# A written order of smaller steps, SyncE's transfers included, for stages 2 and 3 of a two-layer attention and expert kernel

## Chip, cores and metric

One core of one Trainium2 chip. The metric is device microseconds of one launch. Three runs of the kernel before took 717.27 to 718.21 us, median 718.05.

## What is computed

Two rounds over x of 2048 rows and 576 columns, each a linear attention block and then a block of 64 experts, both behind a layernorm and added to x. The reference, cut:

```python
    def _A_ref(x, wqkv, wo):                      # H = 32 heads of 18
        q, k, v = ...(x @ wqkv)
        phi = lambda t: jnp.where(t > 0, t + 1, jnp.exp(t)) + 1e-6
        pq, pk = phi(q), phi(k)
        kv = jnp.einsum("bhsd,bhse->bhde", pk, v)
        z = jnp.einsum("bhsd->bhd", pk)
        o = einsum(pq, kv) / (einsum(pq, z) + 1e-6)
        return o.reshape(B, S, D) @ wo
    def _B_ref(x, w_q, k1, k2, u, v):             # H = 32, E = 8, 64 experts
        s1, s2 = (q1 @ k1.T), (q2 @ k2.T)         # q = x @ w_q, two halves of 128
        top_e = argmax(s1) * E + argmax(s2)       # per row and head
        act = gelu(einsum("nd,nhkd->nhk", x, u[top_e]))
        return einsum("nhk,nhkd->nd", act, v[top_e])
    x = x + _A_ref(_layernorm(x), A_wqkv, A_wo)
    x = x + _B_ref(_layernorm(x), ...)
    (both once more)
```

## The kernel before

The rows are 16 tiles of 128. Every matmul's operands are split into a rounded part `hi` and a remainder `lo` (`split`, L117: ScalarE rounds at L119, VectorE subtracts at L120), so that a product of 576 columns is 28 matmuls.

The work of one tile in one round, by the names that the order uses: `ln` or the end of `po` makes the normalised row; `fT` turns and splits it; `k`, `v`, `q` are products (`product`, L260) with their activations (`phi`, L276; in the second round `phi_scalar`, L283); `st` adds the tile to the state `kva` (L362). When all 16 tiles are in, `wl` loads wo, `mk`, `zs` and `M` mask the state, sum it into `zb` and fold it into wo (L381 to L437). Then per tile: `ld` loads x and phi(q) (L438, L443; parts `ldx`, `ldq`), `num` scales phi(q) (L455 to L465), `oT` turns and splits it, `O` is the output product (L485) with residual (L475) and layernorm (L189 to L207), `bT` turns and splits that, `S` are the expert scores (L527), `gel` and `sel` the gelu and the choice of experts (L541 to L590), `cT` turns the weights, and `po` is the expert output (L609) with residual and, in round one, the next layernorm; it stores x (L617) or the result (L623). In round two `bc` joins `bT` of one tile with `cT` of another. `keep` stores a turned tile to DRAM (L335, L336) and `rl` loads it again (L342, L343) for `lq`, the late q.

Turning goes in one of two ways. `transposed` (L209) uses TensorE (L217) and PSUM. `squares`, for the tiles listed in `SQUARES` (23 of `fT`, 10 of `oT`, 9 of `bT`), turns 32 by 32 squares on VectorE (`moved`, L231), writes them to DRAM (L233), reads them back in four transfers (L239) and splits what arrives.

There are three stages. Stage 1, an ordinary loop, does tiles 0 to 9 of the first `fT` to `st` and folds the expert keys. Stages 2 and 3 are written out by hand. A step of a piece of work is the code between two `yield`s of its generator; `play` reads a text such as `oT0.7x2` (two steps of `oT`, round 0, tile 7) and calls the steps in that order, and `in_order` (L159) then ties every instruction of TensorE, ScalarE, VectorE and GpSimd to the one before it on its engine. SyncE, which issues all DMAs, is not tied: the Tile scheduler chooses its order. The middle of stage 2 is a loop of one text over tiles in pairs (s = 5, 7, 9, 11). Buffers are taken when a step asks for them: four PSUM tiles (one of them the state), four pairs `hi`/`lo`, six `x1`, three `x`, three `y`, four `e` (phi of k and q).

Of the kernel before, what the change touches and what calls it, by code (L numbers as in the profile page):

```python
# [64 lines left out]
def network(ctx, tc, x_in, wqkv, wo, wq_t, k_t, u_t, v2, c_mask, c_mask4, c_ident, c_code, c_code1, c_scale, c_shift, out):  # L65
# [120 lines left out]
    def spread(xt, total, n):  # L186

        m = wk.tile([P, 2], F32, tag="mv", name=f"m{n}")
        nc.gpsimd.tensor_scalar(m[:, 0:1], total, -1.0 / D, 1.0, op0=ALU.mult, op1=ALU.mult)  # L189
        nc.scalar.activation(junk, xt, AF.Square, bias=m[:, 0:1], accum_out=m[:, 1:2])  # L190
        return m

    def layernorm_sum(xt, m, n):
        rs = wk.tile([P, 2], F32, tag="rs", name=f"rs{n}")
        nc.gpsimd.tensor_scalar(rs[:, 0:1], m[:, 1:2], 1.0 / D, EPS_LN, op0=ALU.mult, op1=ALU.add)
        nc.gpsimd.tensor_tensor(rs[:, 0:1], rs[:, 0:1], mhalf, op=ALU.pow)
        nc.gpsimd.tensor_tensor(rs[:, 1:2], m[:, 0:1], rs[:, 0:1], op=ALU.mult)  # L197
        return normalized(xt, rs, n)
# [11 lines left out]
    def transposed(y, n, more=None, tag="t", step=P):  # L210
# [16 lines left out]
    def moved(y, n, step=P):  # L227
# [3 lines left out]
        nc.vector.transpose(r.rearrange("p (j b c) -> p b j c", j=4, b=NB), at)  # L231
        d = dr.tile([P, NB * P], F32, name=f"y_d{n}")
# [9 lines left out]
    def squares(y, n, step=P):  # L242
        g = yield from moved(y, n, step)
        hi, lo = (wk.tile([P, NB, P], F32R, tag="t" + w, name=f"t{w}{n}", bufs=4) for w in ("hi", "lo"))
        yield
        split(g.rearrange("p q (b c) -> p b q c", b=NB), *(x.rearrange("p b (q c) -> p b q c", q=4) for x in (hi, lo)))
        return hi, lo
# [28 lines left out]
    def phi(p, n):  # L276
        e = wk.tile([P, D], F32, tag="e", name=f"e{n}", bufs=4)
        nc.scalar.activation(e, row(p), AF.Exp)  # L278
        nc.vector.tensor_scalar(e, e, 1.0, EPS, op0=ALU.min, op1=ALU.add)  # L279
        nc.vector.scalar_tensor_tensor(e, row(p), 0.0, e, op0=ALU.max, op1=ALU.add)  # L280
        return e

    def phi_scalar(p, n):  # L283
# [4 lines left out]
        nc.scalar.activation(e, e, AF.Exp, scale=-1.0)  # L288
        nc.vector.scalar_tensor_tensor(e, e, EPS, row(p), op0=ALU.add, op1=ALU.add)  # L289
# [13 lines left out]
    def front_k(l, t):  # L303
# [4 lines left out]
        tt["fk", l, t] = (phi_scalar if l else phi)(k, f"k{l}_{t}")  # L308
# [15 lines left out]
    def front_q(l, t):  # L324
# [4 lines left out]
        fq = phi(q, f"q{l}_{t}")  # L329
        nc.sync.dma_start(pq_d[l][t], fq)  # L330

    def front_keep(l, t):

        hi, lo = tt["f", l, t]
        nc.sync.dma_start(hl_d[t][:, 0], hi.bitcast(F32))  # L335
        nc.sync.dma_start(hl_d[t][:, 1], lo.bitcast(F32))  # L336

    def late_load(l, t):
# [3 lines left out]
        nc.sync.dma_start(hi.bitcast(F32), hl_d[t][:, 0])  # L342
        nc.sync.dma_start(lo.bitcast(F32), hl_d[t][:, 1])  # L343
        tt["f", l, t] = hi, lo

    def late_q(l, t):
        q = product(tt["f", l, t], whi, wlo, 0, f"q{l}_{t}")
        yield
        tt["pq", l, t] = phi_scalar(q, f"q{l}_{t}")
# [16 lines left out]
    def wo_load(l, t):  # L366
# [7 lines left out]
        yield  # L374
# [4 lines left out]
    def state_mask(l, t):  # L379
        a = kva.pop(l)  # L380
        nc.scalar.activation(zc, a[:, :4 * 72 + 36], AF.Copy)  # L381
        for h in range(2):
# [63 lines left out]
    def back_load(l, t):  # L446
        back_x(l, t)
        back_pq(l, t)

    def back_scale(l, t):  # L450
# [7 lines left out]
        nc.vector.tensor_reduce(den, o[:, :D].rearrange("p (h e) -> p h e", h=H), axis=AX.X, op=ALU.add)  # L458
        nc.gpsimd.tensor_scalar(den, den, EPS, 1.0, op0=ALU.add, op1=ALU.mult)
# [4 lines left out]
                                r.unsqueeze(2).to_broadcast([P, H, DH]), op=ALU.mult)  # L464
        nc.gpsimd.tensor_copy(o[:, D:D + 56], o[:, D - 56:D])  # L465
        tt["o", l, t] = o

    def back_oT(l, t):
        hi, lo = tt["oT", l, t] = yield from turned("o", l, t, tt.pop(("o", l, t)), HC)
        nc.gpsimd.tensor_copy(lo[96:112, 4], hi[:16, 4].bitcast(F32))  # L470
# [7 lines left out]
    def back_out(l, t):  # L478
# [11 lines left out]
        m = spread(x1, total, "b" + n)  # L490
        yield
        ys["b", l, t] = layernorm_sum(x1, m, "b" + n)
# [18 lines left out]
    def exp_c(l, t):  # L511
# [5 lines left out]
        split(pt[:, :P], hi, lo)  # L517
        tt["c", l, t] = hi, lo

    def exp_scores(l, t):  # L520
# [8 lines left out]
        s = wk.tile([P, D], F32, tag="s", name="s" + n)  # L529
        nc.gpsimd.memset(s[:, :NE], 0.0)  # L530
# [4 lines left out]
    def exp_gelu(l, t):  # L535
# [5 lines left out]
        nc.scalar.activation(g[:, 0], xu, AF.Square, scale=float(np.sqrt(0.044715)))  # L541
        nc.gpsimd.tensor_scalar(g[:, 0], g[:, 0], 1.0, 1.0, op0=ALU.add, op1=ALU.mult)
        nc.gpsimd.tensor_tensor(g[:, 1], g[:, 0], xu, op=ALU.mult)
        yield
        nc.scalar.activation(g[:, 1], g[:, 1], AF.Tanh, scale=GELU_C)
        nc.gpsimd.tensor_scalar(g[:, 1], g[:, 1], 1.0, 0.5, op0=ALU.add, op1=ALU.mult)
# [53 lines left out]
    def exp_out(l, t):  # L600
# [13 lines left out]
        else:  # L614
            x2, total = residual(p, xs.pop(("b", l, t)), n, "x2")
        if l == 0:
            nc.sync.dma_start(x_d[t], x2)  # L617
# [62 lines left out]
    def first_ln(l, t):  # L680
        xt = xs.pop(("f", t))
        *_, rs = statistics(xt, f"f0_{t}")
# [22 lines left out]
    def load_vu(l, t):  # L705
        sv = stage("vst")
        nc.sync.dma_start(sv[:64], v2)
        nc.sync.dma_start(sv[64:], v2)
        su = stage("ust")[:, :NB * NE].rearrange("p (b e) -> p b e", b=NB)
# [76 lines left out]
    with in_order(*ALL):  # L786
# [46 lines left out]
        for t in range(2, FIRST):  # L833
# [3 lines left out]
            if t == 2:  # L837
                first_load(0, 4)
                first_ln(0, 3)
# [13 lines left out]
            first_ln(0, t + 2)  # L853
# [5 lines left out]
    with in_order(*ALL):  # L859

        play("""
            fT0.11 v0.10 k0.10 fl0.13 v0.10 q0.10 ln0.13 v0.10 ln0.12 fT0.11x2 fT0.12 fl0.15 k0.10 fo0.3x2 lv0.0 q0.10
            v0.11 fT0.13 fT0.12 k0.11 v0.11x2 wl0.0 q0.11 ln0.15 k0.11 st0.11 fl0.14 fT0.13 st0.10 fT0.12 q0.11 ld0.1
            ln0.14 k0.12x2 v0.12x2 ld0.0 v0.12 fT0.13 q0.12 q0.13 fT0.14 q0.12 k0.13 fT0.14 v0.13 fT0.15 fT0.14 fT0.15
            k0.14 q0.13 k0.13 v0.13 fT0.15 k0.14 v0.13 st0.12 v0.14 k0.15 v0.15 st0.13 ld0.2 v0.14x2 st0.14 k0.15
            sv0.0 v0.15x2 st0.15 ld0.3 mk0.0 zs0.0x2 num0.0 M0.2x2 num0.1 M0.3x2 q0.14 num0.0 num0.1 M0.1 num0.0 oT0.0
            num0.1 M0.0 M0.4 oT0.1 M0.1 oT0.0 M0.0 M0.4 O0.0 num0.2x2 oT0.1 O0.0x3 ld0.4 num0.2 O0.1x2 oT0.2 ld0.5
            num0.3 bT0.0 num0.4 oT0.2 O0.2 ld0.6 num0.3 bT0.0 O0.1 S0.0 num0.3 num0.4 q0.14 O0.1 oT0.3 O0.2 S0.0 bT0.1
            O0.2 q0.15 gel0.0 num0.4 sel0.0 oT0.3 bT0.1 ld0.7 sel0.0x2 O0.2 S0.1 gel0.0 q0.15 num0.5 sel0.0 S0.1
            sel0.1 gel0.1 O0.3 gel0.1 sel0.1 cT0.0 bT0.2 cT0.0 O0.3 oT0.4 po0.0x2 bT0.2 sel0.1 S0.2 po0.0 oT0.4 O0.4  # L870
            sel0.1 S0.2 cT0.1 sel0.2 po0.0 sel0.2 fT1.0 gel0.2 cT0.1 fT1.0 O0.3 po0.1 gel0.2 sel0.2 po0.1 O0.3 v1.0
            sel0.2 cT0.2 po0.1 bT0.3 O0.4x2 cT0.2 k1.0 v1.0 po0.1 v1.0 fT1.1 num0.5 num0.6 bT0.3 k1.0 S0.3 po0.2 fT1.1
            po0.2 S0.3 sel0.3 keep1.0 sel0.3 k1.1 gel0.3 sel0.3 gel0.3 po0.2 k1.1 v1.1 O0.4 bT0.4 sel0.3 cT0.3 po0.2
            v1.1x2 fT1.2 num0.5 cT0.3 bT0.4 oT0.5 fT1.2 num0.6 oT0.5 S0.4x2 keep1.1 num0.6 oT0.6x2 O0.5 keep1.2 po0.3
            O0.5x3 st1.0 st1.1
        """)
    with in_order(*ALL):
# [8 lines left out]
    with in_order(*ALL):  # L886

        play("""
            bT0.13 gel0.12 po0.11 sel0.12 v1.10 po0.11x2 gel0.12 num0.15 sel0.12 k1.10 bT0.13 v1.10 sel0.12 fT1.11
            sel0.12 oT0.14 v1.10 fT1.11 O0.14 num0.15 cT0.12 num0.15 k1.10 cT0.12 O0.14 oT0.15 bT0.13 po0.12 S0.13  # L890
            O0.14 fT1.11 S0.13 oT0.15 po0.12x3 sel0.13x2 v1.11 gel0.13 fT1.12 gel0.13 oT0.15 O0.14 sel0.13x2 k1.11
            v1.11 O0.15 fT1.12 O0.15 bT0.14 st1.10 cT0.13 v1.11 bT0.14 S0.14 cT0.13 O0.15 fT1.12 keep1.12 po0.13 k1.11
            S0.14 gel0.14 sel0.14 po0.13 gel0.14 st1.11 po0.13 k1.12 sel0.14x2 po0.13 fT1.13 k1.12 O0.15 v1.12x2
# [74 lines left out]
```

## Time and profile before

| | |
|---|---|
| median of three runs | 718.05 us |
| the profiled execution | 716.96 us |
| its span | 715.1 us |
| busy: TensorE, VectorE, ScalarE, GpSimd | 698.0, 467.9, 321.7, 202.4 us |
| mean granted TensorE clock | 0.997 |
| moved by DMA | 107.17 MB, 150 GB/s mean |

In the profile PE is TensorE, PEld its weight loads, DVE VectorE, ACT ScalarE, POOL GpSimd and SPq SyncE's queue. An operand's name loses its buffer number: `thio` is a `hi` tile of `oT`, `go` the squares read back for it, `y_do` their copy in DRAM, `ppo` the PSUM of O. "Idle before" is the time in which an engine did nothing ahead of an instruction, with what ended it. A row of the waits gives total, number of times and longest in us. A row of the chain of waits or of the timeline gives start, duration and what ran.

### The profile page before, as it was taken

The numbers are of one execution on the slowest core, as the hardware profiler recorded it, in microseconds if no ns is written. First come the engines' busy times: TensorE is split into PE (matmuls) and PEld (weight loads), VectorE is DVE, ScalarE is ACT, GpSimd is POOL, SyncE is SP. The second block draws the span as 40 slices with busy tenths as digits, with TensorE's granted clock in tenths as the row PEclk, the third lists the DMA queues.
The fourth block names the chain that finished last, engine by engine and source line by source line (L and its number), as shares of the span: only waits on it lengthen the run. The fifth ranks groups of instructions, "written<-read, shape, count | busy, mean of one in ns | idle before, by whom it ended". The sixth has DMA issues, their size and how long they took to land.

```text
span 715.1 us, 14670 instructions
## 1 busy us (share of the span) xinstructions
PE 698.0 (98%) x5464; PEld 650.7 (91%) x5464; DVE 467.9 (65%) x1005; ACT 321.7 (45%) x658; POOL 202.4 (28%) x544
## 2 busy tenths in 40 slices
PE   9999999999999999999999999999999999999995
PEld 6999989999998899889998999999899999999984
DVE  5533342435436876688877888552647788987986
ACT  5422432343224547455555555544543544444443
POOL 2211000111004533333443433210224244433441
PEclk9999999999999999999999999999999999999998
DMA  9848878775302322566767675513632324121101
GB/s 269 293 153 255 267 229 264 247 196 176 108 1 53 114 91 93 166 209 210 233 207 241 216 220 175 165 53 100 176 98 82 123 71 137 45 73 34 67 17 66
DMA packets 82711, 107.17 MB, mean 150 GB/s; under 512 B 8976, under 2 KB 47376, under 8 KB 82640
## 3 DMA queue, kind: packets, MB, share of 16 engines
q1 hardware_dynamic: 82640, 106.24, 47.5%
q8 instruction: 43, 0.70, 0.4%
q14 instruction: 28, 0.23, 0.1%
HBM read 68.88 MB, written 37.32 MB: 149 GB/s over the span
## 4 chain that ended last, share of the span: by engine, by line
PE 79%; DVE 8%; ACT 4%; DMA 3%; issue 3%; POOL 1%; SPq 1%; DVEq 0%; ACTq 0%; POOLq 0%
PE ppq L260 15%; PE ppk L260 13%; PE ppo L485 13%; PE ppv L260 12%; PE pps L527 8%; PE kva L527 4%; PE kva L362 2%; PE fold_ps L641 2%; PE ptb L217 2%; PE po L609 2%; DMA go<-y_do 1%; PE m L416 1%; PE pto L217 1%; DVE x L475 1%; PE ppq L272 1%
## 5 line engine op out<-in xcount | busy, mean ns | idle before, releaser
L485 PE MATMUL ppo<-ohi,thio 126*128 126x252 f32 (+1 forms) x320 | 50.7, 301 | 4.5 <-ACT thio L119 4.4
L485 PEld LDWEIGHTS ppo<-ohi,thio 126*128 126x128 f32 (+1 forms) x320 | 44.9, 189 | 6.2 <-ACT thio L119 5.1
L260 PE MATMUL ppk<-whi,thif 128*128 128x252 f32 (+1 forms) x300 | 45.3, 298 | 0.8 <-ACT thif L119 0.8
L455 POOL TENSOR_TENSOR o<-pq,zb 128x576 f32<-128x576 f32 x19 | 27.4, 1443 | 62.5 <-ACT zb L401 58.7
L190 ACT ACTIVATE junk<-x,mb 128x576 bf16<-128x576 f32 x32 | 24.8, 775 | 45.0 <-POOL mb L189 44.9
L260 PE MATMUL ppv<-whi,thif 128*128 128x252 f32 (+1 forms) x300 | 44.7, 296 | 0.2 <-ACT thif L119 0.2
L260 PEld LDWEIGHTS ppk<-whi,thif 128*128 128x128 f32 x300 | 40.9, 188 | 4.0 <-issue 2.9
L181 POOL TENSOR_SCALAR rsf<-mvf 128x1 f32<-128x1 f32 x16 | 3.4, 212 | 145.3 <-DVE mvf L178 145.2
L207 ACT ACTIVATE yb<-x,rsb 128x640 f32<-128x640 f32 x32 | 29.5, 922 | 33.2 <-POOL rsb L197 33.2
L260 PE MATMUL ppv<-whi,tlof 128*128 128x252 f32 (+1 forms) x300 | 43.9, 293 | 0.0
L260 PE MATMUL ppk<-whi,tlof 128*128 128x252 f32 (+1 forms) x300 | 43.9, 293 | 0.0
L260 PEld LDWEIGHTS ppv<-whi,thif 128*128 128x128 f32 x300 | 41.4, 188 | 1.1 <-issue 0.4
L260 PEld LDWEIGHTS ppk<-whi,tlof 128*128 128x128 f32 x300 | 41.2, 188 | 0.0
L260 PEld LDWEIGHTS ppv<-whi,tlof 128*128 128x128 f32 x300 | 41.2, 188 | 0.0
L485 PE MATMUL ppo<-olo,thio 126*128 126x252 f32 (+1 forms) x256 | 39.6, 293 | 0.0
L260 PE MATMUL ppq<-whi 128*128 128x252 f32 (+1 forms) x260 | 39.5, 298 | 0.0
L485 PE MATMUL ppo<-ohi,tloo 126*128 126x252 f32 (+1 forms) x256 | 39.5, 293 | 0.0
L279 DVE TENSOR_SCALAR ek<-ek 128x576 f32<-128x576 f32 x16 | 7.3, 457 | 45.8 <-ACT ek L278 45.6
L260 PEld LDWEIGHTS ppq<-whi 128*128 128x128 f32 x260 | 36.0, 188 | 0.6 <-DVE eq L289 0.3
L485 PEld LDWEIGHTS ppo<-olo,thio 126*128 126x128 f32 x256 | 36.2, 188 | 0.0
L485 PEld LDWEIGHTS ppo<-ohi,tloo 126*128 126x128 f32 x256 | 36.1, 188 | 0.0
L260 PE MATMUL ppk<-wlo,thif 128*128 128x252 f32 x240 | 36.1, 293 | 0.0
(211 smaller groups left out, 1776.2 us busy)
## 6 DMA issues: line engine op xcount, KB each, us to landing
fold<-in_wq_t SPq DMA_DIRECT2D x64, 288.0 KB
whi<-hl_d SPq DMA_DIRECT2D x26, 320.0 KB
y_df<-rf SPq DMA_DIRECT2D x23, 320.0 KB
gf<-y_df SPq DMA_DIRECT2D x92, 80.0 KB
pq_d<-eq SPq DMA_DIRECT2D x19, 288.0 KB
pq<-pq_d SPq DMA_DIRECT2D x19, 288.0 KB
xf<-in_x SPq DMA_DIRECT2D x16, 288.0 KB
x<-in_x SPq DMA_DIRECT2D x16, 288.0 KB
```

Of the source, the lines that this page charges most:

```text
L190: nc.scalar.activation(junk, xt, AF.Square, bias=m[:, 0:1], accum_out=m[:, 1:2])
L207: nc.scalar.activation(y, x2, AF.Identity, scale=rs[:, 0:1], bias=rs[:, 1:2])
L217: nc.tensor.transpose(pt[:, b * P:(b + 1) * P], x, ident)
L260: nc.tensor.matmul(o[:, at:at + c1 - c0], tt[a == "lo"][:, b, :], wb[:, cols + c0:cols + c1], start=(i == 0), stop=(i == len(todo) - 1))
L272: nc.tensor.matmul(p[:, at:at + c1 - c0], tt[a == "lo"][:, b, :], wb[:, cols + c0:cols + c1], start=(i == 0), stop=(i == len(todo) - 1))
L279: nc.vector.tensor_scalar(e, e, 1.0, EPS, op0=ALU.min, op1=ALU.add)
L362: nc.tensor.matmul(a[64 * h:64 * h + 64, c * 72:c * 72 + n], vt[:, 2 * c + h], fk[:, f0:f0 + n], start=(t == 0 and c == 0), stop=(t == NT ...
L455: nc.gpsimd.tensor_tensor(o[:, :D], pq, zb, op=ALU.mult)
L485: nc.tensor.matmul(p[:, at:at + c1 - c0], hl[a][:r, b], w[:r, c0:c1], start=(i == 0), stop=(i == len(todo) - 1))
L527: nc.tensor.matmul(p[:, :512], hl[a == "lo"][:, b, :], shi[:, b] if w == "hi" else slo[:, blocks(REM)[b][1]], start=(i == 0), stop=(i == l ...
L609: nc.tensor.matmul(p[:, at:at + c1 - c0], c[i], vmix[:, c0:c1], start=(i == 0 and not based), stop=(i == 1))
L641: nc.tensor.matmul(p[32 * j:32 * j + 32, at:at + c1 - c0], kpad[:, ch // 2, 24 - 8 * a:56 - 8 * a], st[:, c0:c1], start=(a == 0), stop=(a ...
```

## The change

Helpers get a second kind of yield, `yield 1`, at which a step can be cut further: between ScalarE's and VectorE's half of a split (`halved` takes the place of `split`), between a VectorE and a GpSimd instruction, before each DMA. `run` passes over these unless `fine` is set, which only `play` does, so stage 1 keeps its steps. The buffers of a split are taken behind the yield, not before it. The three texts of stages 2 and 3, the loop among them, become one text without a loop, in the smaller steps, with the same pieces of work; `SQUARES` stays. `in_order` now also ties SyncE, so DMAs go in the written order. The new order was made with every operand's writers taken into account.

The diff, cut to its core:

```diff
+    def halved(src, hi, lo):
+
+        nc.scalar.activation(hi, src, AF.Copy)
+        yield 1
+        nc.vector.tensor_tensor(lo, src, hi.bitcast(F32), op=ALU.subtract)
+
...
         nc.gpsimd.tensor_scalar(m[:, 0:1], total, -1.0 / D, 1.0, op0=ALU.mult, op1=ALU.mult)
+        yield 1
         nc.scalar.activation(junk, xt, AF.Square, bias=m[:, 0:1], accum_out=m[:, 1:2])
         return m
...
         hi = wk.tile([P, nb, P], F32R, tag=tag + "hi", name=f"thi{n}", bufs=4 if tag == "t" else 1)
         lo = wk.tile([P, nb, P], F32R, tag=tag + "lo", name=f"tlo{n}", bufs=4 if tag == "t" else 1)
-        yield
-        split(pt[:, :w], hi.rearrange("p a b -> p (a b)")[:, :w], lo.rearrange("p a b -> p (a b)")[:, :w])
+        yield from halved(pt[:, :w], hi.rearrange("p a b -> p (a b)")[:, :w], lo.rearrange("p a b -> p (a b)")[:, :w])
         return hi, lo
...
         nc.vector.transpose(r.rearrange("p (j b c) -> p b j c", j=4, b=NB), at)
+        yield 1
         d = dr.tile([P, NB * P], F32, name=f"y_d{n}")
         nc.sync.dma_start(d, r)
...
         yield
-        fq = phi(q, f"q{l}_{t}")
+        fq = yield from phi(q, f"q{l}_{t}")
+        yield 1
         nc.sync.dma_start(pq_d[l][t], fq)
...
         nc.sync.dma_start(hl_d[t][:, 0], hi.bitcast(F32))
+        yield 1
         nc.sync.dma_start(hl_d[t][:, 1], lo.bitcast(F32))
...
             tiles.append(st)
-        yield
+            yield 1
...
     def back_load(l, t):
         back_x(l, t)
+        yield 1
         back_pq(l, t)
...
         nc.vector.tensor_reduce(den, o[:, :D].rearrange("p (h e) -> p h e", h=H), axis=AX.X, op=ALU.add)
+        yield 1
         nc.gpsimd.tensor_scalar(den, den, EPS, 1.0, op0=ALU.add, op1=ALU.mult)
...
+        yield 1
         nc.gpsimd.tensor_copy(o[:, D:D + 56], o[:, D - 56:D])
...
         hi, lo = tt["oT", l, t] = yield from turned("o", l, t, tt.pop(("o", l, t)), HC)
+        yield 1
         nc.gpsimd.tensor_copy(lo[96:112, 4], hi[:16, 4].bitcast(F32))
...
         yield
-        m = spread(x1, total, "b" + n)
-        yield
-        ys["b", l, t] = layernorm_sum(x1, m, "b" + n)
+        m = yield from spread(x1, total, "b" + n)
+        yield
...
+        yield 1
         if l == 0:
             nc.sync.dma_start(x_d[t], x2)
             yield
-            m = spread(x2, total, "f" + n)
+            m = yield from spread(x2, total, "f" + n)
             yield
-            ys["f", 1, t] = layernorm_sum(x2, m, "f" + n)
+            ys["f", 1, t] = yield from layernorm_sum(x2, m, "f" + n)
         else:
...
     def first_ln(l, t):
         xt = xs.pop(("f", t))
-        *_, rs = statistics(xt, f"f0_{t}")
+        st = statistics(xt, f"f0_{t}")
+        next(st)
+        yield 1
+        rs = next(st)
+        yield 1
...
-    def run(l, *seq):
+    def run(l, *seq, fine=False):
 
 
         for f, t, *n in seq:
             if f is bc or ok(t):
                 g = begun.pop((f, l, t), None) or (exp_T(l, *t) if f is bc else f(l, t))
                 for i in range(n[0] if n else 99):
-                    if g is None or next(g, bc) is bc:
+                    e = bc if g is None else next(g, bc)
+                    while e == 1 and not fine:
+                        e = next(g, bc)
+                    if e is bc:
                         break
                 else:
                     begun[f, l, t] = g
...
-            run(int(l), (pieces[f], (at + int(t), at + int(c)) if c else at + int(t), int(n or 1)))
+            run(int(l), (pieces[f], (at + int(t), at + int(c)) if c else at + int(t), int(n or 1)), fine=True)
...
-                first_ln(0, 3)
+                run(0, (ln, 3))
...
-    with in_order(*ALL):
+    with in_order(*ALL, ET.SP):
...
-        for s in range(5, 13, 2):
-            play("""
-            bT0.0 num0.2 po0.-2 sel0.-1x3 gel0.-1 po0.-2x2 v1.-3 gel0.-1 v1.-3 k1.-3 bT0.0 fT1.-2 oT0.1 num0.2 ld0.3
-            sel0.-1 num0.2 k1.-3 bT0.0 fT1.-2 O0.1 cT0.-1 S0.0 O0.1 oT0.2 cT0.-1 po0.-1 O0.1 fT1.-2 num0.3 v1.-3
-            po0.-1 S0.0 O0.1 po0.-1 keep1.-2 v1.-2 po0.-1 gel0.0 k1.-2 gel0.0 st1.-3 sel0.0 bT0.1 sel0.0 oT0.2 v1.-2x2
-            num0.3 ld0.4 fT1.-1 bT0.1 sel0.0x2 fT1.-1 oT0.2 num0.3 oT0.3 k1.-2 O0.2x2 bT0.1 st1.-2 fT1.-1 cT0.0 S0.1
-            keep1.-1 O0.2 cT0.0 O0.2 po0.0 oT0.3 S0.1
-        """, s)
...
-            sel0.12 oT0.14 v1.10 fT1.11 O0.14 num0.15 cT0.12 num0.15 k1.10 cT0.12 O0.14 oT0.15 bT0.13 po0.12 S0.13
...
-            sel0.14 v1.12 bT0.15 cT0.14x2 st1.12 fT1.13 bT0.15 po0.14 S0.15 po0.14 fT1.13 S0.15 po0.14 ldx1.1 po0.14
...
-            po0.15 k1.13 q1.13 bT0.-1 po0.15 q1.13 v1.14 po0.15x2 v1.14 k1.14 wl1.0 st1.13 fT1.15x2 k1.14 k1.15 v1.15
...
-            gel1.12 po1.10 bc1.-1,11x2 base1.12 sel1.12x2 po1.10 sel1.12 po1.11x2 bc1.-1,12x2 po1.12x2
...
+            lv0.0 fl0.13 fo0.3 fT0.11x2 wl1.0 ln0.12 fl0.14 fT0.11 fl0.15 ln0.12x2 ln0.13x2 lv0.0 ld0.1 v0.10 k0.10
...
+            O0.6x3 bT0.5 sel0.4x2 k1.2 bT0.5 k1.2 num0.8x2 k1.2 cT0.4x3 S0.5 fT1.3 S0.5 fT1.3 po0.4x2 O0.6x2 bT0.6
+            S0.5 oT0.7 po0.4x3 gel0.5 sel0.5 bT0.6 num0.8 oT0.8x2 po0.4 oT0.7 po0.4 bT0.6 oT0.7 fT1.4x2 sel0.5 oT0.7
+            v1.3 ld0.10 gel0.5x2 ld0.9 v1.3 fT1.4 v1.3 sel0.5 O0.7x2 k1.3 gel0.5 sel0.5 cT0.5 bT0.6 cT0.5 O0.7x2 st1.2
+            k1.3 bT0.6 O0.7x2 cT0.5 po0.5x2 ld0.9 k1.3 fT1.4 keep1.3 bT0.7 num0.10 S0.6x3 num0.10 keep1.3 gel0.6x2
+            fT1.4 v1.4 gel0.6 sel0.6x3 bT0.7 po0.5x4 oT0.8 po0.5 fT1.5 num0.10 oT0.8 num0.9x2 v1.4 gel0.6 oT0.8
...
+            po0.7 k1.6 po0.7x2 v1.5 po0.7 num0.11 S0.8 sel0.8 po0.7 fT1.7 oT0.10 gel0.8 bT0.9 gel0.8x2 oT0.10 num0.11
+            sel0.8 ld0.12 oT0.10 fT1.7 sel0.8 k1.6 oT0.11 v1.6 bT0.9 gel0.8 sel0.8 v1.6x2 fT1.7 num0.12 k1.6 O0.10x2
+            oT0.11 bT0.9x2 O0.10 keep1.4 num0.12 ld0.13 cT0.8x3 num0.12x3 O0.10x2 oT0.12 S0.9 st1.5 S0.9 fT1.7x2 po0.8
+            S0.9 gel0.9 oT0.11 q0.15 po0.8 oT0.12 O0.10 bT0.10 po0.8 gel0.9 oT0.11 gel0.9 bT0.10 po0.8x3 v1.7x3
+            oT0.11x2 O0.11 ld0.13 po0.8 k1.7 bT0.10x2 gel0.9 sel0.9x2 num0.13 fT1.8x3 sel0.9x2 cT0.9 st1.6 oT0.12
+            O0.11x4 num0.13x2 bT0.10 num0.13 S0.10x2 num0.13 cT0.9x2 po0.9 fT1.8x2 v1.8 po0.9x3 O0.11 S0.10 gel0.10
...
+            fT1.10 bT0.12 O0.13x2 oT0.14x2 st1.8 st1.9 S0.12x2 po0.11x2 O0.13x2 num0.15 O0.13 bT0.13 num0.15 fT1.10
+            po0.11x2 fT1.10 S0.12 sel0.12x3 gel0.12 v1.10 bT0.13 po0.11x2 fT1.11 gel0.12 oT0.14x2 v1.10x2 gel0.12x2
+            keep1.7 k1.10 sel0.12 cT0.12x2 oT0.14x2 O0.14 k1.10x2 bT0.13 cT0.12 bT0.13x2 num0.15x2 fT1.11x3 num0.15
...
+            po0.15x2 st1.12 v1.14 po0.15x4 st1.13 v1.14 k1.14x3 fT1.15x2 q1.13 fT1.15 keep1.10 k1.15x2 v1.15x2 rl1.0
+            rl1.1 v1.15 st1.14 k1.15 st1.15 q1.13x2 mk1.0x2 rl1.0 lq1.0 M1.2 lq1.0 rl1.2 lq1.0 M1.2 zs1.0 M1.3x2 zs1.0
...
+            S1.11 sel1.11 gel1.11 bc1.12,10x3 S1.12x2 gel1.11 sel1.11 base1.12 sel1.11 gel1.11x2 sel1.11 bc1.-1,11
+            po1.15 S1.12 gel1.12 base1.11 sel1.12x2 gel1.12x2 base1.10 po1.10x2 sel1.12 bc1.-1,11x2 po1.11 gel1.12
+            sel1.12 bc1.-1,12x3 po1.12 po1.11 po1.10 po1.11 po1.12x2
```

More of the change, by code (lines that the diff above doesn't have):

```diff
@@ L243, in squares @@
         g = yield from moved(y, n, step)
+        yield
         hi, lo = (wk.tile([P, NB, P], F32R, tag="t" + w, name=f"t{w}{n}", bufs=4) for w in ("hi", "lo"))
-        yield
-        split(g.rearrange("p q (b c) -> p b q c", b=NB), *(x.rearrange("p b (q c) -> p b q c", q=4) for x in (hi, lo)))
+        yield from halved(g.rearrange("p q (b c) -> p b q c", b=NB), *(x.rearrange("p b (q c) -> p b q c", q=4) for x in (hi, lo)))
         return hi, lo
@@ L307, in front_k @@
         yield
-        tt["fk", l, t] = (phi_scalar if l else phi)(k, f"k{l}_{t}")
+        tt["fk", l, t] = yield from (phi_scalar if l else phi)(k, f"k{l}_{t}")
     def front_pair(f, cols, parts=PARTS):
@@ L348, in late_q @@
         yield
-        tt["pq", l, t] = phi_scalar(q, f"q{l}_{t}")
+        tt["pq", l, t] = yield from phi_scalar(q, f"q{l}_{t}")
     def front_state(l, t):
@@ L489, in back_out @@
         yield
-        m = spread(x1, total, "b" + n)
+        m = yield from spread(x1, total, "b" + n)
         yield
-        ys["b", l, t] = layernorm_sum(x1, m, "b" + n)
+        ys["b", l, t] = yield from layernorm_sum(x1, m, "b" + n)
     def exp_T(l, t, c):
@@ L516, in exp_c @@
         yield
-        split(pt[:, :P], hi, lo)
+        yield from halved(pt[:, :P], hi, lo)
         tt["c", l, t] = hi, lo
@@ L681, in first_ln @@
         xt = xs.pop(("f", t))
-        *_, rs = statistics(xt, f"f0_{t}")
+        st = statistics(xt, f"f0_{t}")
+        next(st)
+        yield 1
+        rs = next(st)
+        yield 1
         ys["f", 0, t] = normalized(xt, rs, f"f0_{t}")
@@ L852, in network @@
             run(0, (k, t), (v, t, 1))
-            first_ln(0, t + 2)
+            run(0, (ln, t + 2))
             if done is not None:
@@ new lines, in network @@
+            num1.13 O1.1 oT1.2x2 num1.13 rl1.4x2 O1.1 lq1.4 num1.13x2 oT1.13x2 lq1.3 num1.3 oT1.2 bc1.0,-9 S1.0
+            num1.3x4 oT1.2 O1.1 ldx1.4 bc1.1,-9x2 oT1.13 S1.0x2 sel1.0 oT1.13 lq1.4 bc1.1,-9 O1.2x3 gel1.0x3 S1.1x2
+            gel1.0 keep1.10 oT1.3 rl1.6 ldx1.13 lq1.4 num1.4 S1.1 sel1.0 rl1.7 O1.2 num1.4 sel1.0x2 O1.13 ldx1.5
+            num1.4 lq1.6 O1.2x2 gel1.1 oT1.3 gel1.1 bc1.2,0x2 rl1.10 O1.13 gel1.1 ldx1.3 rl1.7 O1.13x2 sel1.1 gel1.1
+            sel1.1x3 O1.13 lq1.6 lq1.5x2 bc1.2,0 S1.2 lq1.6 O1.13 S1.2 num1.4x2 S1.2 gel1.2 ldx1.9 lq1.5 num1.5
```

115 lines of the change are left out of this document (67 added, 48 removed).

## The prediction

> **What bounds the kernel now.** I read the page first, then busy time by stretches, then what TensorE waited for, then the chain of waits inside the loop of stage 2, then SyncE's own timeline there, and last the chain at the end.
>
> ```profile
> span 715.1 us, 14670 instructions
> ...
> PE 698.0 (98%) x5464; PEld 650.7 (91%) x5464; DVE 467.9 (65%) x1005; ACT 321.7 (45%) x658; POOL 202.4 (28%) x544
> ...
> L260 PE MATMUL ppk<-whi,thif 128*128 128x252 f32 (+1 forms) x300 | 45.3, 298 | 0.8 <-ACT thif L119 0.8
> ```
>
> TensorE is busy for 698.0 of 715.1 us, so everything that a new order of the same instructions could give lies in the 17.1 us between the two. The change adds no instruction and drops none, so the 698.0 stays. Where the gaps lie, the next two views say. In the stretches the columns are PE, PEld, DVE, ACT and POOL busy time, the clock and the DMA share.
>
> ```profile
> 300.00:350.00 50.00, 47.36 (x355) 44.69 (x353) 41.67 (x89) 28.97 (x62) 20.19 (x54) 1.00 0.68 219
> 350.00:400.00 50.00, 48.26 (x390) 45.61 (x390) 39.16 (x84) 28.02 (x57) 19.66 (x50) 1.00 0.70 214
> ```
>
> ```profile
> PE ppo L485 <- ACT thio L119: 4.4, 4, 1.4
> PE ptb L217 <- DVE cg L590: 2.5, 1, 2.5
> ...
> PE ppk L260 <- ACT thif L119: 0.8, 1, 0.8
> PE z L398 <- ACT zc L381: 0.6, 1, 0.6
> PE po L609 <- DVE ek L289: 0.6, 1, 0.6
> PE kva L362 <- ACT g L541: 0.5, 1, 0.5
> ```
>
> In 100 us of the loop TensorE is idle for 2.64 + 1.74 = 4.4 us, and the largest wait of the list, four waits of the output product O for `thio`, the split of its turned operand, is 4.4 us too. The second row is the end of the kernel, where the last tile's choice of experts has nothing left to run beside. The chain of one of the four waits:
>
> ```profile
> 363.76 3.64 PE ppk L260 x28
> 367.40 3.70 PE ppo L485 x28
> ...
> 371.20 3.21 PE kva L527 x14
> 374.41 0.55 PE po L609 x4
> ...
> 379.53 3.77 DMA go<-y_do
> ...
> 383.41 0.74 ACT thio L119
> ...
> 384.20 3.94 PE ppo L485 x28
> ```
>
> Matmuls flow back to back until O of tile 11 at 384.20 has to wait for a transfer that reads the turned square back from DRAM. SyncE's timeline says why that transfer is late:
>
> ```profile
> 372.68 0.32 SPq L233 DMA_DIRECT2D y_do<-ro  x1
> ...
> 377.23 0.32 SPq L239 DMA_DIRECT2D go<-y_do  x1
> 377.64 0.38 SPq L617 DMA_DIRECT2D x_d<-x  x1
> 378.07 0.42 SPq L239 DMA_DIRECT2D go<-y_do  x1
> 378.59 0.42 SPq L233 DMA_DIRECT2D y_db<-rb  x1
> 379.06 2.49 SPq L239 DMA_DIRECT2D go<-y_do  x2
> ```
>
> The square is written at 372.68. Its four reads start 4.55 us later, and they are not issued together: the queue's order, which this kernel doesn't write down, puts a store of x and another tile's write between them, so that the last is issued at 381.55, 4.3 us after the first. The trip from the write's issue to `thio` at 383.41 takes 10.7 us.
>
> **The change part by part.** *The four O waits.* In the old text of the loop, between `oT` (the DVE transpose that starts the trip) and O of tile 11 TensorE has po of 8, v and k of 7 and one state update: 0.55 + 3.64 + 3.64, 7.8 us without the small groups. In the new text v of 6, O of 10, S of 9, po of 8 and v of 7 lie between: 3.64 + 3.70 + 3.21 + 0.55 + 3.64 = 14.7 us. Tiles 7 and 9 are moved likewise. The trip with the split behind it takes 384.20 - 372.68 = 11.5 us, so these three are covered with about 3 us over. The four reads of one tile are now one step of a written queue, which also takes the 4.3 us between first and last read towards four issues of 0.42, but I count no gain for that beyond the wait. Tile 6, at the loop's entry, has in the new text nearly the work that it had; for it I count half of the longest wait, 0.7. So 4.4 - 0.7 = 3.7 us of idle goes. A pause costs a little more than its idle time: a matmul is shown with 298 ns, but back to back they start 3.64 / 28 = 0.13 us apart, so 0.17 us of overlap is lost at each. With 3.5 pauses that is 0.6, together 4.3 us.
>
> *Three single waits.* po of 12 waited 0.6 us for the DVE, because the split of its operand stood behind the end of a phi; the new text puts O of 14, 3.70 us, between that transpose and po. The state update of tile 11 (0.5) waited for the evacuation of its k; k and v of 12, 7.3 us, now stand between besides what stood there. k of 15 (0.8) followed its own transposes directly; q of 13 now stands between. With 0.17 each: 0.8 + 0.7 + 1.0 = 2.5 us less. The wait of z (0.6) stays: in both texts z follows the last state update directly. What is late next in these places is again TensorE, which has no other waits there.
>
> *What the new order adds.* Three expert outputs of the loop (tiles 5, 6, 10) have only one small group between the transpose of their weights and po. The end of the kernel shows that chain bare:
>
> ```profile
> 703.72 0.61 ACT s L532
> ...
> 709.46 0.34 PE ptb L217
> ...
> 710.16 1.19 PE po L609 x4
> 711.42 0.65 ACT x L613
> ```
>
> It takes 710.16 - 709.46 = 0.70 us; the state update in between covers some of it, so each such place costs from nothing to 0.7; I take 0.2 each, 0.6 us. The choice of experts, bare, takes 709.46 - 703.72 = 5.7 us. For tile 12 the new order leaves v and k of 10 behind the scores, 7.3 us, where the old text had v, k and O; the DVE has other work for 41.67 of 50 us in such a stretch, so that place costs from nothing to the whole chain, 5.7, if the DVE takes it up last. A row of equal kind is near: the 0.6 for which po waited on DVE. I take 0.7. At the end the store of tile 11 moves: its copy out of PSUM now stands behind the last transpose's split on ScalarE, and its DMA goes directly ahead of the last one. The last copy ends at 711.42 + 0.65 = 712.07 and the span ends 3.0 us later, so two such stores close together cost between nothing and another 3.0; they overlap on 16 engines, so I take 0.5. Sum of the additions: 1.8 us.
>
> *Edits at nothing.* Yields within a helper, the later allocation of hi and lo, `first_ln` as a generator: the same instructions in stage 1, under TensorE's products. wo's first chunk for the second half, loaded at the start of stage 2, takes one of six x1 buffers until then; in the new text x1 of tile 7 lives from O of 7 past O of 8 and 9 to po of 7, three at once, so five suffice. If they didn't, the residual would wait and PSUM with it.
>
> *The queue of SyncE.* It now runs in the written order with everything in it, loads, keeps, stores and turns. Behind a store that waits for its producer stand the reads of the next square, behind those ScalarE's split, and behind that O. That is where a loss would come from:
>
> ```profile
> SPq L335 <- ACT thif L119: 23.0, 9, 7.2
> ```
>
> In the old order the store of a kept `thif` held the queue for 7.2 us at worst and 23.0 / 9 = 2.6 us on average over nine times.
>
> [...]
>
> **Sum.** -4.3 - 2.5 + 1.8 = -5.0 us. The profiled execution took 716.96 us around its span of 715.1, and I expect 712.0 around 710.1. The median of the runs before is 718.05, 1.1 above the profiled one, so the median after is 713.05; I say 713.0.
>
> **The rivals.**
>
> *The gain goes further.* All 4.4 us go, the additions fit: with 0.17 at four pauses 5.1, and 2.5, and about one more from pauses under 0.4 us: 8.6 less, 709.5 us. For it: the trips have 3 us over. Against: the DVE is 83% busy in the loop.
>
> *The waits move to the DVE, no change.* TensorE stops waiting for transfers and starts waiting for choices and splits queued on the DVE. The bare chain of 5.7 us becomes critical if half a microsecond of other DVE work too much lies in it, for ten tiles: 10 x 0.5 = 5.0, 718.05 us. For it: 41.67 of 50. Against: TensorE's list shows one wait for the DVE in the middle of the kernel, 0.6 us. That the written order doesn't take effect gives the same time: the scheduler still chooses buffers, so a wait for a buffer could undo it; little speaks for that.
>
> *Slower: SyncE held in front of the reads.* In the loop each of ten O trips has about 3 us over. A hold longer than that ahead of the reads shows in full. If the average hold of 2.6 us comes twice in a trip, 5.2 - 3 = 2.2 us are lost each time, ten times 22; even in one trip of three it is 7 us, and the time 718.05 - 6.8 + 1.8 + 7 = 720.0. It decides from holds of 3 us. For it: a written order can't let a ready read pass a store that is not. [...] Against: the reads were late in an order that nobody wrote, and the new one leaves other work between write and reads.
>
> **How the numbers follow.** A measurement of this kernel can tell about 0.2% from no change, 1.4 us: same is 716.6 to 719.5. I give my forecast (710.5 to 716.5) 0.55, the larger gain 0.18, no change 0.14 and slower 0.13. Faster is 0.73. The range goes from 708.5, one below the larger gain, to 719.5, the end of the case of no change, and leaves out the slower case and a little below.
>
> **What would show it.** In the profile after, the waits of ppo for `thio` from the loop are gone or below 1 us in sum, the four reads of a square stand together in SyncE's timeline, and TensorE is busy for over 49 of 50 us between 300 and 400. TensorE's busy time stays near 698. New waits of po, and of transposes for cg, sum to under 2 us. The forecast is wrong if ppo still waits for DMA, if new waits for the DVE appear in most tiles, or if the last 20 us grow by more than 1.

## The result and the profile after

| | before | after |
|---|---|---|
| median of six runs each | 717.66 us | 712.77 us (711.80 to 713.93) |
| ratio | | 0.9923, 95% interval 0.9897 to 0.9949 |
| the profiled execution, around its span | 716.96, 715.1 us | 712.88, 711.1 us |

Faster by 4.9 us of the medians, where 5.0 was forecast. The sum was close; both of its terms were too small, and the errors partly cancel.

From the page of after: span and busy time, and the group of O's matmuls, whose last column is the idle time ahead of them.

```profile
span 711.1 us, 14610 instructions
...
PE 695.5 (98%) x5464; PEld 649.1 (91%) x5464; DVE 466.2 (66%) x1005; ACT 321.3 (45%) x658; POOL 202.2 (28%) x544
...
L504 PE MATMUL ppo<-ohi,thio 126*128 126x252 f32 (+1 forms) x320 | 50.5, 300 | 0.1
```

What TensorE waited for in after, the longest first, and the stretches of stage 2:

```profile
PE kva L546 <- DVE tlob L126: 1.9, 1, 1.9
PE ppk L269 <- ACT thif L124: 1.4, 1, 1.4
PE po L631 <- ACT thib L124: 1.3, 2, 0.9
...
PE ptf L225 <- DVE yf L213: 1.1, 1, 1.1
PE ptf L225 <- ACT yf L215: 1.1, 1, 1.1
...
PE z L413 <- ACT zc L395: 0.6, 1, 0.6
...
PE ptb L225 <- DVE cg L612: 0.2, 1, 0.2
PE po L631 <- DVE tlob L126: 0.2, 1, 0.2
```

```profile
300.00:350.00 50.00, 50.00 (x379) 47.64 (x378) 41.31 (x88) 29.64 (x61) 20.32 (x54) 1.00 0.66 211
350.00:400.00 50.00, 50.00 (x392) 47.39 (x390) 40.42 (x85) 27.20 (x57) 21.80 (x52) 1.00 0.70 222
400.00:450.00 50.00, 48.13 (x365) 44.53 (x364) 36.04 (x81) 28.46 (x62) 16.65 (x48) 1.00 0.56 175
```

O waits for nothing any more, and TensorE is busy for 100 of 100 us where it lost 4.4. The single waits of po, of the state update and of k are gone too. In stages 2 and 3 two waits stand that I had not named: one at 404.24, one at 173.70. The chains of both, the first with one of its SyncE steps (start, duration, what ran):

```profile
395.80 3.15 DMA y_df<-rf
...
399.00 0.32 SPq L248
...
400.79 2.35 DMA hl_d<-tlof
...
403.36 0.84 DVE tlob L126
...
404.24 1.45 PE kva L546 x5
```

```profile
171.80 0.27 POOL rsf L189
...
172.10 0.02 ACT yf L215
...
172.93 0.73 ACT thif L124
...
173.70 2.35 PE ppk L269 x16
```

At 404.24 the scores wait for `tlob`, whose buffer is held by a kept `tlof` until its store (`hl_d`) is done, and in the written order that store stands behind the reads of another square, which wait 3.15 us for their own write. At 173.70 a k waits for a split that stands on ScalarE behind the normalisation of another tile, which waits for GpSimd's statistics.

A place that both kernels have splits the time: the first z, at the end of stage 2's first part. Before and after:

```profile
212.91 0.72 PE L398 MATMUL z<-zc,pick 128*128 128x288 f32 x2 [0.63 <-ACT zc L381]
```

```profile
215.55 0.72 PE L413 MATMUL z<-zc,pick 128*128 128x288 f32 x2 [0.63 <-ACT zc L395]
```

From z to the end before took 715.1 - 212.91 = 502.2 us, after 711.1 - 215.55 = 495.6: the gain is 6.6 us there, and 2.6 us are lost ahead of z. The new wait at 173.70 is 1.4 of that (1.5 with the lost overlap). The other 1.1 comes almost all from stage 1, whose instructions are the same: its second turn starts at 9.26 us, in before at 8.53, because VectorE gets the second tile of x later (its statistics begin at 6.22, in before at 5.49), and where the two orders part, at 155.75 us in before and 156.71 in after, the new kernel is 1.0 behind. The waits of these first turns differ from run to run (1.1 each in after, 0.6 and 0.4 in the fastest kernel below), so I don't put this 1.0 down to the new order.

### The profile page after: what moved, and what is told of

The parts are those of the page before. It is cut to its first block, busy times and chain, and to the rows that moved or that the text cites. A ratio compares the mean times of both kernels' runs of the same rounds, so it can differ in the third digit from the quotient of the medians.

```text
span 711.1 us, 14610 instructions
## 1 busy us (share of the span) xinstructions
PE 695.5 (98%) x5464; PEld 649.1 (91%) x5464; DVE 466.2 (66%) x1005; ACT 321.3 (45%) x658; POOL 202.2 (28%) x544
## 4 chain that ended last, share of the span: by engine, by line
PE 81%; DVE 7%; DMA 4%; issue 2%; ACT 2%; SPq 1%; POOL 1%; DVEq 0%; ACTq 0%; POOLq 0%
PE ppo L504 15%; PE ppq L269 15%; PE ppk L269 13%; PE ppv L269 13%; PE pps L546 8%; PE kva L546 4%; PE kva L376 3%; PE fold_ps L664 2%; PE po L631 2%; PE ptb L225 2%; DMA y_df<-rf 2%; PE pto L225 1%; PE m L431 1%; PE ppq L281 1%; DMA xf<-in_x 1%
## 5 line engine op out<-in xcount | busy, mean ns | idle before, releaser
L269 PE MATMUL ppv<-wlo,thif 128*128 128x252 f32 x240 | 36.1, 293 | 0.0
```

The source lines that it names most:

```text
L269: nc.tensor.matmul(o[:, at:at + c1 - c0], tt[a == "lo"][:, b, :], wb[:, cols + c0:cols + c1], start=(i == 0), stop=(i == len(todo) - 1))
```

## The experiments

Theory T1 was the prediction's: O's waits go because more products lie between oT and O, and the single waits go for the same reason. R1: it is SyncE's written order, which issues a square's four reads together. R2: it is the smaller steps. A fourth question was what VectorE's load costs. Each kernel is told with its ratio to before and the interval.

**SyncE's order alone taken away** (from after).

```diff
-    with in_order(*ALL, ET.SP):
+    with in_order(*ALL):
```

> The kernel after, with SyncE's order left to the scheduler again; the other four engines keep the new order. Theory (T1): the gain comes from the products that the new order puts between oT and O, and from the three single waits; the trips themselves did not become shorter. Then most of the gain stays: 713 to 715 us, and O waits for thio under 1 us in sum in the middle of the kernel; the store of the kept lo part may even go earlier, which would give back the 2.0 us at 404.24. Rival (R1): the gain comes from SyncE's written order, which issues a square's four reads together. Then the split reads come back and with them the waits of O: 716 to 718 us, ppo waiting 3 us or more for thio.

712.20 us, ratio 0.9929 (0.9910 to 0.9948), the same as after. O waits in no place of TensorE's list. SyncE's own timeline, here for tile 11, has the four reads together without being tied. Why the scheduler does so here and not in before is not shown: the reads are one step of the text in both.

```profile
366.82 0.43 SPq L242 DMA_DIRECT2D y_do<-ro  x1
...
369.58 1.75 SPq L248 DMA_DIRECT2D go<-y_do  x4
```

R1 falls in its plain form: tying SyncE gives nothing that the order of the other engines has not given.

**SyncE tied in the old loop** (from before; the text is unchanged).

```diff
-    with in_order(*ALL):
+    with in_order(*ALL, ET.SP):
         for s in range(5, 13, 2):
```

> The kernel before with one word more: SyncE is tied to the old text within the loop of stage 2 (five trips of the text, 10 tiles), so the four reads of a square are issued together and in the text's place. R1: O's waits in the loop shrink by the 2 to 2.5 us by which the reads are together, to zero: 4 to 5 us less than before, 713 to 714. T1: the reads were held back by what stands ahead of them as much as by what came between; the text that was not made for SyncE holds it at stores and keeps: between 1 us faster and 10 us slower, 717 to 728, with new waits on DMA.

722.55 us, ratio 1.0079 (1.0058 to 1.0099). O waits more than before, not less:

```profile
PE ppo L485 <- ACT thio L119: 6.3, 7, 1.4
```

So an order of SyncE made from a text that was written for the other engines costs. (The old text as a whole with SyncE tied was not tried.)

**After, with less work between oT and O** (tiles 7, 9, 11). Pieces of the text; the last three lines are the places they move to:

```diff
-oT0.7 po0.3 oT0.7 bT0.5
-oT0.9 fT1.5 oT0.8 O0.8x2
-oT0.11 v1.6 bT0.9 gel0.8
+cT0.4x3 oT0.7x3 S0.5
+cT0.6 oT0.9x3 po0.6
+oT0.12 oT0.11x3 S0.9
```

> The kernel after, with the first three steps of the O trip (transpose, write, reads) of tiles 7, 9 and 11 moved behind some 7 us of products, so that about as much is left between oT and O as in the kernel before. SyncE stays tied and the four reads stay together. T1: the three waits come back, 1 to 1.5 us each: 3 to 4.5 us above after, 715.8 to 717.2, with ppo waiting for thio again. R1: reads that go together make the trip short enough, no wait comes back: 712.8, same as after. In between (trip shortened by the 2 to 2.5 us by which the reads are together): one us or less in sum, 713.5.

723.01 us, ratio 1.0084 (1.0065 to 1.0103), 10.2 above after: more than either theory said, in T1's direction. O waits again, for long in two of the three tiles, 7 and 11 (5.6 us in TensorE's list). The chain of the longer one, tile 11, and two stretches of this kernel:

```profile
377.35 0.81 DVE ro L239
...
378.18 2.11 DMA y_do<-ro
...
381.65 2.00 DMA go<-y_do
...
383.67 0.74 ACT thio L124
...
384.46 6.51 PE ppo L504 x28
```

```profile
378.00:384.00 6.00, 3.32 (x26) 3.09 (x24) 2.39 (x5) 1.01 (x2) 1.16 (x3) 0.94 0.50 164
384.00:390.00 6.00, 5.54 (x23) 5.54 (x24) 5.28 (x13) 2.89 (x8) 2.99 (x7) 0.50 0.71 237
```

Here the trip is short: the reads stand directly behind the write, and it takes 383.67 - 378.18 = 5.5 us to the split, half of the 10.7 of before. O is late all the same, because the trip starts late: VectorE reaches the turn only at 377.35. And behind the wait of 3.1 us the granted clock is 0.50 for the next 6 us, so that O takes 6.51 us instead of 3.70, 2.8 more. What decides is when the turn starts, ahead of the products that cover it; this is T1, with a price per microsecond that the expectation had too low.

**Before, with the turn of the loop's odd tiles put earlier**, in two places:

```diff
-sel0.-1 num0.2 k1.-3 bT0.0 fT1.-2 O0.1 cT0.-1 S0.0 O0.1 oT0.2 cT0.-1
+sel0.-1 num0.2 oT0.2 k1.-3 bT0.0 fT1.-2 O0.1 cT0.-1 S0.0 O0.1 cT0.-1
```

> The kernel before, with one step moved in the text of the loop: the DVE transpose that begins the trip of the odd tiles' O operand (oT0.2) goes from behind the first two steps of O and the scores to directly behind the operand's last num step, about 8 us of products earlier. Nothing else is changed, SyncE is not tied. T1: the four waits of O (4.4 us, 5.1 with the lost overlap) are the largest term and go, all but tile 6 or so: 3 to 4.5 us less than before, 713 to 714.7. R1 (SyncE's order is what matters): the write goes earlier but the reads are still issued late and apart, O still waits 3 us or more, 716.5 to 718. R2 (the finer steps give the gain): no change, 717 to 718.

718.43 us, ratio 1.0018 (1.0006 to 1.0031): no gain at all, slightly slower, where T1 had expected 713 to 714.7. TensorE's list for it:

```profile
PE ptc L514 <- DVE ek L289: 2.6, 4, 1.0
...
PE ppo L485 <- ACT thio L119: 1.4, 1, 1.4
```

Three of O's four waits are gone, as T1 says. Four new ones of the turned weights `ptc` have come. On VectorE in one trip of the loop:

```profile
336.29 0.29 DVE L590 TENSOR_TENSOR cg<-g,ct 128x128 f32<-128x128 f32 x1
...
337.97 0.85 DVE L231 STREAM_TRANSPOSE ro<-o 128x640 f32<-128x640 f32 x1 [0.33 <-POOL o L465]
338.74 0.72 DVE L289 SCALAR_TENSOR_TENSOR ek<-ek,ppk 128x576 f32<-128x576 f32 x1
```

```profile
339.51 0.33 PE L514 MATMUL ptc<-ident,cg 128*128 128x128 f32 x1 [0.46 <-DVE ek L289]
```

`cg`, what ptc turns, was there at 336.58. ptc waits for `ek`, which reads k's product out of PSUM, and starts when that ends, at 339.46: by that I read it as waiting for the PSUM tile. The turn `ro` now stands ahead of `ek`. In before the same `ek` ended 0.6 us ahead of `ptc`, at 338.22:

```profile
337.47 0.75 DVE L289 SCALAR_TENSOR_TENSOR ek<-ek,ppk 128x576 f32<-128x576 f32 x1
```

```profile
338.81 0.27 PE L514 MATMUL ptc<-ident,cg 128*128 128x128 f32 x1
```

So the edit itself made this wait: the turn takes 0.85 us of VectorE ahead of `ek`, more than the 0.6 that was to spare. That gave T2, that it would work with ek first:

```diff
-sel0.-1 num0.2 oT0.2 k1.-3 bT0.0
+sel0.-1 num0.2 k1.-3 oT0.2 bT0.0
```

> The kernel before with the same step of its loop (oT0.2, the transpose that begins the trip) moved less far than in the run before: behind the next step of k, and so behind the DVE half of phi (ek), which empties the PSUM tile of k, but still ahead of the split of bT, of the two steps of O and of the scores. New theory (T2): in the old loop the DVE's queue stood behind the O waits; the transpose put ahead of ek held a PSUM tile, for which the turned weights ptc then waited (2.6 us), and that ate the gain. With ek ahead of it ptc waits for nothing and the O waits stay short: 2 to 3.5 us less than before, 713.5 to 715. Rival: the waits only move on, to the split of bT and the residual of O, which the transpose still delays by 0.8 us each trip: no change or slower, 716 to 718.5.

723.11 us, ratio 1.0087 (1.0067 to 1.0107). T2 falls; its rival, that the waits only move on, is right in kind, but in another place than it said, and the time is above its range too. ptc has no wait in the list any more, O keeps the one of tile 6 (1.4) and one of 0.4, and the scores wait for the turned row of the expert block:

```profile
PE kva L527 <- ACT thib L119: 4.4, 4, 1.4
```

```profile
346.81 1.56 SPq L335 DMA_DIRECT2D hl_d<-thif  x1
348.46 0.38 SPq L336 DMA_DIRECT2D hl_d<-tlof  x1
348.90 0.45 SPq L617 DMA_DIRECT2D x_d<-x  x1
349.44 0.56 SPq L233 DMA_DIRECT2D y_db<-rb  x1
```

On SyncE, in the order that the scheduler chose, two stores of a keep and one of x now stand ahead of the write `y_db`, whose square was ready at 346.17 + 0.84 = 347.0, so the write starts 2.4 us late. In before it started at 346.06, at once behind its square, and the split `thib` was done 1.7 us ahead of the scores. In the old loop, then, these two operands are ready only 0.6 and 1.7 us ahead of their use, and each edit delayed one of them by more than that. Neither kernel got faster, but neither takes O's wait away and leaves all else as it was; what that alone would give in the old loop stays open.

**After, with the halves of computing steps joined**, R2's test: the cuts inside split, phi, num, gelu and statistics are passed over, so that the second half goes at the place of the first. In the helpers and in `run`:

```diff
-        yield 1
+        yield 2
...
-                    while e == 1 and not fine:
+                    while e == 2 or e == 1 and not fine:
                         e = next(g, bc)
+                        left -= 1
```

> The kernel after with the new cuts inside computing steps taken out in all of stages 2 and 3: the two halves of a split, of phi, of num and of the gelu go together again, each at the place of its first half; the cuts ahead of DMAs stay, and the order of everything else is the same. R2 (the finer steps are what gives the gain): 2 us or more above after, 715 to 718, with waits for DVE on TensorE's list. T1 and T2 (the order of the large steps gives it): 712 to 714, no new wait of over 1 us in the middle of the kernel.

818.36 us, ratio 1.1403 (1.1382 to 1.1424), some 100 us above both expectations. The other side, the first half moved to the place of the second, by the text alone, with SyncE untied:

```diff
-fT0.12x2 v0.10x2 ln0.13 k0.10x2 fo0.3 fT0.13 fT0.11 q0.10x2 fT0.11 v0.11
+fT0.12x2 v0.10x2 ln0.13 k0.10x2 fo0.3 fT0.13 q0.10 fT0.11x2 v0.11
```

> The other side of the run with joined halves: the halves of a split, of phi, of num and of the gelu go together again, now each at the place of its second half, so that ScalarE or VectorE does the first half later than in the kernel after (up to some tens of steps later). SyncE is left to the scheduler, so the time is to be held against the run with SyncE free, 712.2. If the place of the second half alone is what VectorE's queue needs, 712 to 718. If both places count, as the 818 us with both halves at the first place suggest, 725 us or more, with TensorE waiting for ScalarE's halves (thio, thif, thib) instead of cg and o.

868.58 us, ratio 1.2098 (1.2070 to 1.2126). The longest wait in the list of each:

```profile
PE ptc L533 <- DVE cg L612: 21.5, 9, 4.9
```

```profile
PE ppo L504 <- ACT thio L124: 39.0, 15, 4.3
```

With the second half too early TensorE waits for VectorE's results, with the first half too late for ScalarE's splits. Part of the time is the clock: its mean was 0.967 and 0.942, in after 0.997, which over 814 and 869 us is about 24 and 48. So the new order can't simply be played without the cuts: each engine in turn must find its half where its operand is ready. This does not say that coarse steps can't do well: before had them at 717.66. How much of the gain the smaller steps give (R2) is therefore not shown. Which of the cuts matters was not tried, nor was the later allocation of hi and lo.

**More work for VectorE**, 16 instructions of 0.42 us (6.7 us in all; the first maximum of the choice done twice in round one, same result), in after and in before:

```diff
-        nc.vector.tensor_tensor(mt, s[:, :256], s[:, 256:512], op=ALU.max)
+        for _ in range(2 if l == 0 else 1):
+            nc.vector.tensor_tensor(mt, s[:, :256], s[:, 256:512], op=ALU.max)
```

> The kernel after with the first maximum of the choice of experts done twice in the first round (same result): 16 instructions of 0.42 us more on VectorE, 6.7 us in all, about ten of them in the loop. If VectorE decides the loop's pace in the new order, its waits grow by 3 to 7 us, 716 to 720. If TensorE alone is the bound and the new order leaves VectorE slack, at most 1 us more, 712.8 to 714.

> The kernel before with the same 16 instructions of 0.42 us more on VectorE (first maximum of the choice done twice in the first round, same result). In the kernel after they cost 3.7 us, 0.55 of their own 6.7 us. If the new order has used up slack of VectorE that the old one had, less here: 0 to 2 us, 717 to 719. If the old loop already ran at VectorE's pace, as much or more: 4 to 7 us, 721 to 724.

After with it: 716.44 us, ratio 0.9987 (0.9976 to 0.9997), 3.7 above after. Before with it: 719.07, ratio 1.0026 (1.0011 to 1.0041), 1.1 above before in its own comparison. The same work costs more in the new order. But part of the 3.7 is the clock: the wait at 404.24 has grown to 2.6 us, and in the stretch behind it the clock is 0.71, which over 5.8 us is 1.7. The 2.0 that are left are near the 1.1 of before, so that the new order leaves VectorE much less room is not shown.

```profile
406.20:412.00 5.80, 5.80 (x42) 4.99 (x43) 3.89 (x10) 3.68 (x8) 1.98 (x6) 0.71 0.42 109
```

**The two new waits taken out of after**, first each by itself:

```diff
-num0.14 S0.11 gel0.10 keep1.6 sel0.10
+num0.14 S0.11 gel0.10 sel0.10
-fT1.6 oT0.10 keep1.6 O0.9x2
+fT1.6 oT0.10 keep1.6x2 O0.9x2
```

> The kernel after with one step moved: the store of the lo part of the kept turned tile 6 (second step of keep1.6) directly behind the store of its hi part. Nothing else is changed. If the wait of the scores for tlob at 404.24 (2.0 us) is SyncE's hold of that store and nothing else: 2.0 less than after, 710.8. If another wait takes its place: 712 to 713.

```diff
-sv0.0 fT0.12 ln0.14x3 fT0.12 fT0.13
+sv0.0 fT0.12 ln0.14x2 fT0.12 ln0.14 fT0.13
```

> The kernel after with one step moved: the last step of the normalisation of tile 14, at the beginning of stage 2, goes behind the step of fT of tile 12 that splits it. If the wait of k of 12 at 173.70 (1.5 us) is ScalarE held by that step and nothing else: 1.5 less than after, 711.3. If it moves on: 712.3 to 713.

710.70 us (ratio 0.9905, 0.9887 to 0.9924) and 710.86 (0.9909, 0.9891 to 0.9926). In each the wait that was meant is gone from TensorE's list and the other is still there:

```profile
PE ppk L269 <- ACT thif L124: 1.4, 1, 1.4
```

```profile
PE kva L546 <- DVE tlob L126: 2.3, 1, 2.3
```

The first of the two fences is the run with the store moved, the second that with ln moved. Both together, with the second store of every keep behind its first:

> The kernel after with two of its new waits taken out: the second step of each keep (the store of the lo part) directly behind the first, for all tiles, so that the store of tile 6 no longer stands behind the reads of a later square; and the last step of the normalisation of tile 14 in stage 2's beginning behind the last step of fT of tile 12, whose split waited 1.5 us for it. If the two stalls (2.0 at 404.24, 1.5 at 173.70) are worth what they show: 3.5 us below after, 709.3. If SyncE only holds other reads instead, or the next wait takes the place: 711.5 to 713.

709.63 us, ratio 0.9895 (0.9880 to 0.9910): the lowest time of this study. Its longest wait in TensorE's list is the one at the end of the kernel:

```profile
PE po L631 <- ACT thib L124: 1.3, 2, 0.9
```

The three medians are 2.1, 1.9 and 3.1 below after's, 2.0, 1.5 and 3.5 were expected. By the ratios, each to the kernel before measured beside it, they are only 1.3, 1.0 and 2.0 us below after. The intervals still overlap after's, so the sizes rest on the waits that are gone more than on the times.

## Why the prediction was right, step by step

**The four O waits (-4.3).** All four went, tile 6's too, for which I had counted half: 4.4 of idle and four times 0.17, 5.1 us. The mechanism is the one put down, more products between the turn and O, and the kernel with fewer products there shows it from the other side. Reads that go together are not what did it: in that kernel they go together too, and O waits. In the working, the last read of before is put at 381.55, where a row of two issues ends; the chain has it at 379.53, 2.3 us behind the first and not 4.3. No term rests on it. That the trips are covered "with about 3 us over" was wrong as an account of the queue, for the trips differ widely in after. Tile 11's and 12's on SyncE:

```profile
367.54 0.38 SPq L242 DMA_DIRECT2D y_do<-ro  x1
...
370.49 1.74 SPq L248 DMA_DIRECT2D go<-y_do  x4
...
373.62 0.34 SPq L242 DMA_DIRECT2D y_do<-ro  x1
...
385.44 1.73 SPq L248 DMA_DIRECT2D go<-y_do  x4
```

Tile 12's reads are issued 11.8 us behind the write, and nobody waits for them: the order starts that trip long before it is needed. Reads go together, as I said they would, yet they are not early.

**What is late next.** The sentence "What is late next in these places is again TensorE, which has no other waits there" held in after: no wait of 0.3 us or more came up where the seven had been. But the working never asked how long the operands that come next had been ready, and a list of waits doesn't show that. The two kernels with the turn put earlier show that it matters: with 0.6 or 1.7 us to spare, a delay of 0.85 or 2.4 made new waits of 0.5 to 1.4 us, like O's. That the new order keeps clear of them in the loop, but for the one at 404.24, is shown; which of its moves does it is not.

**Three single waits (-2.5).** Gone, at the size put down: neither po for `ek` nor the state update for `g` nor k of 15 for `thif` is in the list of after, and that of z stayed at 0.6. I gave no term to the 2.5 us for which the last tile's `ptb` waited on `cg`. That wait went to 0.2, but others took its place near the end, so little came of it.

**The additions (+1.8).** Half of the real sum, and in the wrong places. The three po behind short chains, tile 12's choice and the close stores cost next to nothing: the list has no wait of po or `ptc` in stage 2 (its waits of po and the 0.2 for `cg` lie in the last 26 us), and from the last product to the end it is 3.8 us in both kernels. What the order did add is 1.4 + 1.9 us of waits, 3.6 with 0.17 of lost overlap at each, at two places that I had not looked at: a split on ScalarE behind ln, and a store on SyncE behind other reads. The second is my slower rival, SyncE held, at one place instead of one trip in three. Together -5.1 - 2.5 + 3.6 = -4.0, the change of the span, where I had -6.8 + 1.8 = -5.0; the slower start is about +1.0, and small waits that came and went make up for it. Both of my terms were too small, by 0.8 and by 1.8, and the errors partly cancel: that the medians differ by 4.9 where I said 5.0 is in part luck.

**Edits at nothing.** The cuts are not at nothing in stages 2 and 3; I had weighed them as a change to stage 1 alone. The new order needs them (818 and 869 us without); what they cost or give by themselves was not run.

**The rivals.** The larger gain, 709.5, is what this order gives once its two new waits are mended: 709.63. The waits did not move to VectorE in after. How near that rival was stays open: 6.7 us more of VectorE's work cost 3.7 us, 1.7 of it by the clock. In the page TensorE's busy time fell to 695.5, where I held 698.0 fixed. Of these 2.5 us, 1.5 are no work of the layers: the 14 products of `warm_up` at the start took 6.16 us in before and 4.64 in after, and the first turn behind them starts at nearly the same time, 7.17 and 6.95. Behind the first product the lists have 12 pauses of 0.3 us or more in before and 7 in after; five less are 0.9 by my own 0.17.

## What to carry to other kernels

Before a wait is priced, look how long ago the operands that come next were ready: 0.6 us here, which an edit that delayed one of them by 0.85 used up. When an order is written by hand, put both halves of each piece of work on each engine's own queue where their operands come ready, start a transfer early enough that products cover it (started late, it kept O waiting for 3.1 us here) but not ahead of what empties a PSUM tile (a turn put there brought 2.6 us of waits for `ek`), and keep a store that frees a buffer ahead of reads that wait for something else (1.9 us at 404.24). After such a change read the new list of waits from the top: here the first two lines were mistakes of one step each, and mending them gave 3.1 us more by the medians, 2.0 by the ratios.

## What the runs showed of the hardware

Behind some pauses of TensorE more was lost than their own length: behind the 3.1 us of O in the kernel with less work in between the granted clock was 0.50 for 6 us (2.8 us lost), and behind 2.6 us in after with more work for VectorE 0.71 over 5.8 us (1.7 lost). Behind the other long wait of O in the first of these, 2.4 us, it was 1.00, and so it was behind the 1.9 us at 404.24 in after. Behind the 2.5 us at the end of before it was 0.50 again, from 710.42 on, so near 2.5 us the length of a wait alone does not tell. The two stretches at 1.00, in this order:

```profile
316.00:320.00 4.00, 4.00 (x32) 4.00 (x32) 3.70 (x9) 1.41 (x5) 1.51 (x5) 1.00 0.45 138
```

```profile
404.00:410.00 6.00, 5.76 (x51) 5.03 (x52) 5.26 (x13) 3.63 (x8) 2.39 (x7) 1.00 0.50 153
```

A square's trip through DRAM with nothing else in SyncE's way, that of tile 11 in the kernel with less work in between, took 5.5 us: 2.1 for the write to land, 1.3 between the first and the last read's issue, 2.0 for the last to land. In the 10.7 us of before the first read is issued 4.6 us behind the write, the last 2.3 behind the first, and it lands 3.8 after that.
